# Four bank pairs for the last products of a two-attention kernel, and one VectorE tile fewer

## The chip, the cores and the metric

The kernel runs on one core of one Trainium2 chip. The metric is device microseconds of one execution. Before the change the median of three runs is 1860.64 us (1858.08 to 1861.57).

## The reference

Two attentions over the same input are mixed by a gate, token by token. Cut to what matters:

```python
B, S, D = 1, 2048, 512; H = 32; Dh = 16
g = sigmoid((x * gate_w).sum(-1))
# a: 32 query heads, one key head and one value head for all
a = softmax(einsum("bhqd,bkd->bhqk", x @ wq, x @ wk) * Dh**-0.5) @ (x @ wv), heads joined, @ wo_a
# b: 32 heads, each with its own keys and values
b = softmax(q @ k.T * Dh**-0.5) @ v per head, heads joined, @ wo_b
out = g * a + (1 - g) * b
```

All of it is float32. There are 2 x 32 heads with 2048 x 2048 scores each, and every score needs one exponential.

## The kernel before

**Work and its units.** The 64 heads form eight groups of eight (`groups`, alternately of a and b). A group has four *phases*: two halves of the tokens by two sets of four heads. A phase has 64 score tiles of 128x1024: PE makes them in 8 matmuls from K and Q tiles (`products`, two PSUM tiles `sc` in turn), and an exponential turns each into probabilities. Most exponentials run on ACT (`score`, tiles `prob`). Some run on VectorE (`chain`): the scores then go into a PSUM bank pair `pair`, and seven VectorE instructions follow, one that converts, two with bit masks, and four of a polynomial in place, on tiles `vec`. A chain holds three `vec` tiles while it runs, and its result stays in one until PE has read it. PE multiplies the probabilities with the values (`values`) into the other bank pair. When a phase is full, VectorE copies that bank pair to `raw` (`emptied`), ten small transfers bring numerators to `oT` and denominators to `dT` (`normalised`), and VectorE divides: a reciprocal (`over`), a multiplication (`times`), and a split into two float16 halves (`high` a cast, `low` a subtraction), which go to `o16`.

**Other products.** Between scores and values PE also works on *units*: projections to q, k and v of later groups, and output products (`o_unit`: four token tiles for each half of a group, 48 matmuls each when both sets of heads are in). An output product is gated by VectorE into a tile `sum` and added to the output in DRAM by POOL's queue. For the last group the output so far is read back into `late`, and VectorE adds the gated product to it in one instruction.

**What sets the order.** A planner in Python (`_Plan`) keeps a clock for each engine and writes the instructions out one by one. PE's next job is a score if ACT can take one, else values, a unit or the scores of a chain. A chain is begun when no unit is pressed for time (`hurry`, from each unit's due time), when enough `vec` tiles are free (`vector_job`), and when the phase has room (`pick`). So a unit that is due later leaves VectorE free for more chains, and each chain takes one exponential from ACT. Each engine then runs its own list in order.

**The end.** The last phase's division and the last output products stand behind the planner's loop, in a list of their own: in four steps of 128 tokens VectorE runs `over` and `times`, ACT `high` and POOL `low`; PE makes 24 matmuls, always into the same bank pair; VectorE adds the two halves of the gated product, and two queues (SP and ACT) store them.

```python
for t in range(4):
    if t < 3:
        c = (t + 1) * P
        over(c), times(c), high(c), low(c)
    for fn, _ in last[t].jobs:
        fn()
    last[t].finish(plan.pe)
```

Of the kernel before, what the change touches and what calls it, by code (L numbers as in the profile page):

```python
# [12 lines left out]
F32 = mybir.dt.float32  # L13
# [7 lines left out]
P = 128  # L21
# [26 lines left out]
TO_VEC, FROM_VEC, CHAINED = 255, 150, 130  # L48
X_JOB = 685
ISSUE, ISSUE_SP, LANDS, SUM_LANDS = 480, 600, 3200, 6500  # L50
PROBS, VECS = 6, 7


@with_exitstack
# [110 lines left out]
def _fast(ctx, tc, x, wq_a, wk_a, wv_a, wo_a, wqkv_b, wo_b, gate_w, out, flag):  # L165
# [36 lines left out]
    def by_tiles(outs, lhs, rhs, start, stop):  # L202


        for n in range(0, P, COLS):
            for i in range(2):
                nc.tensor.matmul(outs[n : n + COLS, i], lhs[i][rows(i), n : n + COLS], rhs[i][rows(i)],  # L207
                                 start=start, stop=stop)
# [122 lines left out]
    def kv_split(h, bank):  # L331


        pk = bank[:, :, : 4 * M].rearrange("p a (i m) -> p a i m", i=4)
        k32 = ops.tile([P, 2, 4, DH], F32, tag="k32", name=f"k32{h}", bufs=1)
        kn = sums[1][:, h].bitcast(F16).rearrange("p (i a b d) -> p i a b d", i=8, a=2, b=4)
        ts = slice(8 * h, 8 * h + 8)

        def take(queue=nc.sync, key=True, value=True):
            if key:  # L340
                nc.vector.tensor_scalar(k32, pk[:, :, :, :DH], UP ** -1, None, op0=ALU.mult)
            if value:
                for d in (0, 2 * DH):
                    v = vA[0][:, ts, d : d + DH].rearrange("p (e i) d -> p e i d", e=2)
                    nc.vector.tensor_scalar(v, pk[:, :, :, DH : 2 * DH], UP ** -2, None, op0=ALU.mult)
                swapped(vA[1][:, ts], vA[0][:, ts], queue)
                nc.vector.tensor_copy(z[:, ts].rearrange("p (e i) -> p e i", e=2), pk[:, :, :, 2 * DH])

        def halve():
            k8 = k32.rearrange("p e i d -> p (e i) d")  # L350
            nc.vector.tensor_copy(kn[:, :, 0, 0, :], k8)
            nc.vector.tensor_tensor(kn[:, :, 0, 2, :], k8, kn[:, :, 0, 0, :], op=ALU.subtract)
            nc.vector.tensor_copy(kn[:, :, 0, 1, :], kn[:, :, 0, 0, :])
            nc.vector.tensor_copy(kn[:, :, 0, 3, :], kn[:, :, 0, 2, :])
            nc.vector.tensor_copy(kn[:, :, 1], kn[:, :, 0])
        def top():
            absmax("k_a", h, k32.rearrange("p e i d -> p (e i) d"), AX.XY)

        return kn, take, halve, top
# [121 lines left out]
    def o_unit(n, half, t, qs, first, last):  # L481

        src, gi = groups[n]
        w, i = weights[src, gi, "o"], "ab".index(src)
        steps = [(q, a, b) for q in qs for a, b in PARTS]
        tt = [8 * half + t, 8 * half + 4 + t]
        mine = late[:, 4 * half + t]
        state = {}

        def job(k):  # L490
            q, a, b = steps[k]
            lhs = [o16s[n, half, q][:, a, t * P : (t + 1) * P]] * 2
            rhs = [w[e ^ (q // 2)][:, b] for e in range(2)]
            by_tiles(pair[1], lhs, rhs, k == 0, k == len(steps) - 1)

        def finish(end):
            def take(e):
                g = gate_up[:, i, tt[e] : tt[e] + 1]
                if n + 1 == len(groups):
                    nc.vector.scalar_tensor_tensor(mine[:, e], pair[1][:, e], g, mine[:, e], op0=ALU.mult, op1=ALU.add)  # L500
                    if last:
                        (nc.sync, nc.scalar)[e].dma_start(out[tt[e] * P : (tt[e] + 1) * P, :], mine[:, e])
                    return
                if e == 0:
                    state["sum"] = sums[state["turn"]]
                nc.vector.tensor_scalar(state["sum"][:, e], pair[1][:, e], g, None, op0=ALU.mult)  # L506

            def then(t):
                free["spare"] = t + FROM_VEC
                if n + 1 == len(groups):  # L510
                    return
                dst = out.rearrange("(h e t p) d -> h t p e d", h=2, e=2, p=P)[half, t_]
                if n == 0:
                    done = plan.on_sp([lambda: nc.sync.dma_start(dst, state["sum"])], t, ISSUE_SP)
                else:
                    done = plan.on_pool([lambda: nc.gpsimd.dma_start(dst, state["sum"], accum_op=ALU.add)], t, 1300)  # L516
                sum_free[state["turn"]] = done + SUM_LANDS

            t_ = t
            begin = end + TO_VEC  # L520
            if n + 1 < len(groups):
                state["turn"] = turn[0]
                turn[0] ^= 1
                begin = max(begin, sum_free[state["turn"]])
            for e in range(2):
                plan.vec(lambda e=e: take(e), 660, 1, begin, (), then if e else None)

        made = ready.get
        jobs = [(lambda k=k: job(k), PRODUCT) for k in range(len(steps))]
        due = 32 * (4 * n + 2 * half + 4)  # L530
        return _Unit(jobs, finish, lambda now: all(made(("o16", n, half, q), math.inf) <= now for q in qs)
                     and made(("wo", src, gi), math.inf) <= now and made("gates", math.inf) <= now
                     and (sum_free[turn[0]] <= now + 4000 if n + 1 < len(groups) else made("late", math.inf) <= now), lambda: starts_in(due), f"o{n}{half}{t}")
# [3 lines left out]
    def normalised(n, half, q, raw, now):  # L537

        src, gi = groups[n]
        ends = n + 1 == len(groups) and half and q  # L540
        o, d = (ops.tile([P, BLK], F32, tag=tag, name=f"{tag}{n}{half}{q}", bufs=1) for tag in ("oT", "dT"))
        queues = (nc.sync, nc.scalar, nc.gpsimd) if ends else (nc.sync,)
        moves = [(d, DH, 2 * DH, 0), (d, 5 * DH, 2 * DH, 2 * DH), (o, 0, DH, 0), (o, 3 * DH, 2 * DH, DH), (o, 7 * DH, DH, 3 * DH)]
        moves = [(*move, e) for part in (0, 2) for e in range(2) for move in moves[part : part + 2 + part // 2]]
        for m, (part, at, n_rows, to, e) in enumerate(moves):
            queues[m % len(queues)].dma_start(part[ROWS * e + to :][:n_rows], raw[at : at + n_rows, e])  # L546
        plan.sp = max(plan.sp, now) + len(moves) * ISSUE_SP
        o16 = ops.tile([P, 2, BLK], F16, tag="o16", name=f"o16{n}{half}{q}", bufs=3)
        o16s[n, half, q] = o16
        cut = P if ends else BLK // 2  # L550

        def over(c):
            nc.vector.reciprocal(d[:, c : c + cut], d[:, c : c + cut])  # L553

        def times(c):
            nc.vector.scalar_tensor_tensor(o[:, c : c + cut], o[:, c : c + cut], UP, d[:, c : c + cut], op0=ALU.mult, op1=ALU.mult)

        def high(c):
            (nc.scalar.copy if ends else nc.vector.tensor_copy)(o16[:, 0, c : c + cut], o[:, c : c + cut])  # L559

        def low(c):
            (nc.gpsimd if ends else nc.vector).tensor_sub(o16[:, 1, c : c + cut], o[:, c : c + cut], o16[:, 0, c : c + cut])

        if ends:
            tail.append((over, times, high, low))
            return
        due = now + 30000

        def then(end):
            ready["o16", n, half, q] = end + FROM_VEC  # L570

        for c in range(0, BLK, cut):
            a = plan.vec(lambda c=c: over(c), 1560, 3.5, now + 7700, (), None, due)
            b = plan.vec(lambda c=c: times(c), 330, 3.4, now + 12000, (a,), None, due)
            e = plan.vec(lambda c=c: high(c), 200, 3.3, 0.0, (b,), None, due)
            plan.vec(lambda c=c: low(c), 330, 3.2, 0.0, (e,), then if c else None, due)
# [132 lines left out]
    def emptied(t):  # L709
# [9 lines left out]

        def take():  # L720
            state["raw"] = ops.tile([P, 2, BLK], F32, tag="raw", name=f"raw{ph}", bufs=1)
            nc.vector.tensor_copy(state["raw"], full)  # L722

        def then(end):
            free[which] = end + FROM_VEC
# [496 lines left out]
        else:  # L1222
            plan.vector()

    over, times, high, low = tail[0]
    last = [o_unit(len(groups) - 1, 1, t, (2,), False, True) for t in range(4)]
    over(0), times(0), high(0), low(0)
    for t in range(4):
        if t < 3:
            c = (t + 1) * P  # L1230
            over(c), times(c), high(c), low(c)
        for fn, _ in last[t].jobs:
            fn()
        last[t].finish(plan.pe)
        for op in plan.ops:
            op.fn()
        plan.ops.clear()


def _sigmoid(nc, gate, z, scale):  # L1240
# [146 lines left out]
```

## Time and profile before

| | |
|---|---|
| median of three runs | 1860.64 us |
| the profiled execution: time, span | 1863.72 us, 1861.9 us |
| mean granted TensorE clock | 0.992 |
| busy: PE, VectorE (DVE), ACT, POOL | 1760.7, 1217.5, 1797.5, 392.0 us |
| exponentials of scores on ACT, on VectorE | 1944, 104 |
| first and last exponential on ACT start at | 32.2, 1829.4 us |

PE is TensorE's matmul, PEld its weight load, a name with q (SPq, ACTq) the sequencer that issues transfers. A number such as L622 is a line of the kernel; a group of rows is named by what it writes and reads, without buffer numbers. In a row of a timeline stand start, length, engine, line, operation, and in brackets the idle time before it with what ended it. Matmuls are pipelined and their ends are modelled, so PE's busy time is more than the work it must do. Idle time of an engine that is not the bottleneck costs nothing.

### The profile page before, as it was taken

Reading aid. Unit: us, or ns where it says so; the run is one execution under the profiler, and the core shown is the slowest. Engines: PE = TensorE matmul, PEld = TensorE weight load, DVE = VectorE, ACT = ScalarE, POOL = GpSimd, SP = SyncE. Lnnn points to the kernel's source line nnn. Section 1 sums busy time; section 2 is a strip of 40 time slices with the busy share of each in tenths; the row PEclk is TensorE's granted clock in tenths of the full one; section 3 lists DMA queues with packets and bytes.
Section 4 is the critical chain, followed back from the end, with each engine's and each line's share of the span. In section 5 each row is a group of like instructions: output and inputs, shape, how many; then the busy total and the mean of one; then the engine's idle time right before and its main releaser. Section 6 shows DMA issues by size and latency. Waiting matters only on the chain.

```text
span 1861.9 us, 97691 instructions
## 1 busy us (share of the span) xinstructions
PE 1760.7 (95%) x45403; PEld 859.8 (46%) x45403; DVE 1217.5 (65%) x1369; ACT 1797.5 (97%) x1959; POOL 392.0 (21%) x575
## 2 busy tenths in 40 slices
PE   9999999999999999999999999999999999998994
PEld 5544454444444444444444445444444444443441
DVE  4267323969686772678677684297868677349963
ACT  4999999999999999999999999999999999999993
POOL 4213103232031211412112320242202320130000
PEclk9999999999999999999999999999999999999997
DMA  5121212223142322412224240252313322234011
GB/s 146 41 60 43 82 32 55 82 57 57 32 79 40 66 49 59 83 35 54 43 50 75 51 80 21 51 97 48 57 40 54 65 53 45 51 66 124 24 49 59
DMA packets 75678, 109.69 MB, mean 59 GB/s; under 512 B 22256, under 2 KB 30672, under 8 KB 75264
## 3 DMA queue, kind: packets, MB, share of 16 engines
q0 software_dynamic: 27904, 44.24, 14.1%
q1 hardware_dynamic: 43920, 56.51, 11.9%
q8 instruction: 357, 5.85, 1.4%
q10 hardware_dynamic: 3440, 2.62, 0.4%
q14 instruction: 57, 0.47, 0.1%
HBM read 14.82 MB, written 33.55 MB: 26 GB/s over the span
## 4 chain that ended last, share of the span: by engine, by line
ACT 74%; PE 11%; issue 8%; DVE 5%; DMA 1%; SPq 1%; POOL 0%; ACTq 0%; DVEq 0%
ACT prob L622 74%; PE pair L663 5%; PE sc L608 3%; DVE vec L828 2%; PE pair L207 2%; DVE vec L816 1%; SPq L546 1%; DVE xT L500 0%; DVE dT L553 0%; DVE sum L506 0%; PE pt L294 0%; PE pair L294 0%; PE pair L457 0%; DVE vec L819 0%; DVE raw L722 0%
## 5 line engine op out<-in xcount | busy, mean ns | idle before, releaser
L622 ACT ACTIVATE prob<-sc 128x1024 f32<-128x1024 f32 x1932 | 1777.0, 1125 | 12.3 <-PE sc L608 10.4
L663 PE MATMUL pair<-prob,vA 64*32 64x512 f32 (+1 forms) x8168 | 521.8, 566 | 0.8 <-issue 0.8
L663 PE MATMUL pair<-prob,vB 64*32 64x512 f32 (+1 forms) x8112 | 521.7, 570 | 0.5 <-issue 0.5
L608 PE MATMUL sc<-Qb,K 64*32 64x512 f16 x7744 | 409.5, 381 | 47.0 <-ACT prob L622 38.7
L608 PE MATMUL sc<-Qa,kA 64*32 64x512 f16 x7808 | 409.5, 381 | 20.4 <-ACT prob L622 12.3
L608 PEld LDWEIGHTS <-K 64*32 64x32 f16 x8192 | 203.8, 90 | 422.9 <-issue 382.9
L608 PEld LDWEIGHTS <-kA 64*32 64x32 f16 x8192 | 202.9, 90 | 390.3 <-issue 349.9
L828 DVE SCALAR_TENSOR_TENSOR vec<-vec,vec 128x1024 f32<-128x1024 f32 x312 | 378.3, 1224 | 2.6
L663 PEld LDWEIGHTS pair<-prob,vA 64*32 64x32 f32 x8168 | 158.7, 105 | 23.7 <-issue 4.8
L663 PEld LDWEIGHTS pair<-prob,vB 64*32 64x32 f32 x8112 | 157.8, 105 | 22.2 <-issue 2.7
L816 DVE TENSOR_SCALAR vec<-pair 128x1024 int32<-128x1024 f32 x104 | 126.4, 1215 | 51.6 <-PE pair L608 49.3
L828 DVE SCALAR_TENSOR_TENSOR vec<-vec 128x1024 f32<-128x1024 f32 x104 | 131.3, 1263 | 1.2
L516 POOL DMA_DIRECT2D out_dram<-sum x48 | 60.1, 1253 | 340.7 <-DVE sum L506 330.8
L553 DVE RECIPROCAL dT<-dT 128x256 f32<-128x256 f32 (+1 forms) x66 | 111.4, 1693 | 28.2 <-DMA dT<-raw 28.2
L722 DVE COPY raw<-pair 128x1024 f32<-128x1024 f32 x32 | 39.2, 1224 | 115.3 <-PE pair L663 115.2
L506 DVE TENSOR_SCALAR sum<-pair,gate_up 128x512 f32<-128x512 f32 x112 | 79.2, 742 | 49.2 <-PE pair L207 49.1
L390 POOL DMA_DIRECT2D K<-hikb x64 | 31.1, 491 | 341.7 <-DVE hikb L431 340.9
L390 POOL DMA_DIRECT2D Qa<-hiqa x63 | 31.9, 511 | 335.7 <-DVE hiqa L431 316.9
L207 PE MATMUL pair<-w16ob,o 64*32 64x512 f16 x1536 | 66.1, 392 | 14.8 <-ACT o L559 6.9
L823 DVE TENSOR_SCALAR vec<-vec 128x1024 int32<-128x1024 int32 x104 | 78.1, 751 | 0.0
L819 DVE TENSOR_SCALAR vec<-vec 128x1024 int32<-128x1024 int32 x104 | 75.2, 723 | 1.4
L431 DVE TENSOR_SCALAR hivb<-pair 128x1024 f16<-128x1024 f32 x8 | 9.8, 1224 | 101.2 <-PE pair L207 101.2
(149 smaller groups left out, 1272.2 us busy)
## 6 DMA issues: line engine op xcount, KB each, us to landing
out_dram<-sum POOLq DMA_DIRECT2D x48, 512.0 KB, 6.1
dT<-raw SPq DMA_DIRECT2D x126, 64.0 KB, 3.0
vB<-vB SPq DMA_DIRECT2D x16, 384.0 KB, 3.8
out_dram<-sum SPq DMA_DIRECT2D x8, 512.0 KB, 3.8
xT<-out_dram SPq DMA_DIRECT2D x16, 256.0 KB, 5.0
oT<-raw SPq DMA_DIRECT2D x126, 32.0 KB, 2.9
oT<-raw SPq DMA_DIRECT2D x62, 64.0 KB, 2.9
vec<-in_A_x_dram SPq DMA_DIRECT2D x14, 256.0 KB, 4.9
```

The lines of the kernel that those rows point to most:

```text
L207: nc.tensor.matmul(outs[n : n + COLS, i], lhs[i][rows(i), n : n + COLS], rhs[i][rows(i)], start=start, stop=stop)
L390: fns.append(lambda q=queues[len(fns) % len(queues)], dst=dst, src=hilo[part][at]: q.dma_start(dst, src))
L506: nc.vector.tensor_scalar(state["sum"][:, e], pair[1][:, e], g, None, op0=ALU.mult)
L516: done = plan.on_pool([lambda: nc.gpsimd.dma_start(dst, state["sum"], accum_op=ALU.add)], t, 1300)
L553: nc.vector.reciprocal(d[:, c : c + cut], d[:, c : c + cut])
L608: nc.tensor.matmul(bank[a : a + COLS, hh], k[rows(hh), key : key + COLS], Q[src, gi, half, p][rows(hh), j * BLK : (j + 1) * BLK], start=Tr ...
L622: nc.scalar.activation(probs[u], sc, AF.Exp, scale=SCALE / (UP * UP))
L663: nc.tensor.matmul(pair[0][32 * k : 32 * k + 32, i, cols], v[rows(i)], probs[2 * m + k // 2][rows(i), hh, cols], start=first, stop=last)
L816: nc.vector.tensor_scalar(tile("p").bitcast(I32), pair[1], SCALE / (UP * UP) / math.log(2) * 2.0 ** 23, None, op0=ALU.mult)
L819: nc.vector.tensor_scalar(tile("m").bitcast(I32), tiles["p"].bitcast(I32), 0x7FFFFF, 125 << 23, op0=ALU.bitwise_and, op1=ALU.bitwise_or)
L823: nc.vector.tensor_scalar(tile("w").bitcast(I32), tiles["p"].bitcast(I32), 0x7F800000, 0x40000000 | LEAD, op0=ALU.bitwise_and, op1=ALU.bit ...
L828: nc.vector.scalar_tensor_tensor(p, m if i == 3 else p, VEC[i], m if i else w, op0=ALU.add, op1=ALU.mult)
```

## The change

Six edits. (1) VectorE's tiles `vec` are six, not seven; the input tiles that had borrowed them at the start use both `sum` tiles, and the scratch for k moves from `sum` to the places of `oT` and `dT`. (2) The due time of each output product is three phases later. (3) `o16` has six places, not three, since they wait longer for their product. (4) `low` runs on VectorE at the end too, not on POOL. (5) The copy of the last phase's bank pair is halved between VectorE and ACT. (6) The last list is written anew: each of the four token tiles has its own bank pair (both `pair` and both `sc`), VectorE's gated sums (`give`) stand between its divisions, and all eight stores go through SP's queue.

```diff
-PROBS, VECS = 6, 7
+PROBS, VECS = 6, 6
...
-        kn = sums[1][:, h].bitcast(F16).rearrange("p (i a b d) -> p i a b d", i=8, a=2, b=4)
+        kn = ops.tile([P, BLK], F32, tag=("oT", "dT")[h], name=f"kn{h}", bufs=1)
+        kn = kn.bitcast(F16).rearrange("p (i a b d) -> p i a b d", i=8, a=2, b=4)
...
-        due = 32 * (4 * n + 2 * half + 4)
+        due = 32 * (4 * n + 2 * half + 7)
...
-        o16 = ops.tile([P, 2, BLK], F16, tag="o16", name=f"o16{n}{half}{q}", bufs=3)
+        o16 = ops.tile([P, 2, BLK], F16, tag="o16", name=f"o16{n}{half}{q}", bufs=6)
...
-            (nc.gpsimd if ends else nc.vector).tensor_sub(o16[:, 1, c : c + cut], o[:, c : c + cut], o16[:, 0, c : c + cut])
+            nc.vector.tensor_sub(o16[:, 1, c : c + cut], o[:, c : c + cut], o16[:, 0, c : c + cut])
...
-            nc.vector.tensor_copy(state["raw"], full)
+            if ph == LASTS:
+                nc.vector.tensor_copy(state["raw"][:, 0], full[:, 0])
+                nc.scalar.copy(state["raw"][:, 1], full[:, 1])
+            else:
+                nc.vector.tensor_copy(state["raw"], full)
...
-    last = [o_unit(len(groups) - 1, 1, t, (2,), False, True) for t in range(4)]
-    over(0), times(0), high(0), low(0)
+    into = [pair[1], pair[0]] + [ps_s.tile([P, ACT, BLK], F32, tag="sc", name=f"end{t}") for t in range(2)]
+
+    def products_of(t):
+        for k, (a, b) in enumerate(PARTS):
+            lhs = [o16s[n, 1, 2][:, a, t * P : (t + 1) * P]] * 2
+            by_tiles(into[t], lhs, [w[e ^ 1][:, b] for e in range(2)], k == 0, k == len(PARTS) - 1)
+
+    def give(t, e):
+        tt, mine = 8 + 4 * e + t, late[:, 4 + t, e]
+        nc.vector.scalar_tensor_tensor(mine, into[t][:, e], gate_up[:, 1, tt : tt + 1], mine, op0=ALU.mult, op1=ALU.add)
+        nc.sync.dma_start(out[tt * P : (tt + 1) * P, :], mine)
+
+    over[0]()
+    times[0]()
     for t in range(4):
-        if t < 3:
-            c = (t + 1) * P
-            over(c), times(c), high(c), low(c)
-        for fn, _ in last[t].jobs:
-            fn()
-        last[t].finish(plan.pe)
-        for op in plan.ops:
-            op.fn()
-        plan.ops.clear()
+        high[t]()
+        if t < 3:
+            over[t + 1]()
+        elif t == 3:
+            give(1, 1)
+            give(2, 0)
+        low[t]()
+        products_of(t)
+        if t < 3:
+            times[t + 1]()
+        if t == 1:
+            give(0, 0)
+        if t == 2:
+            give(0, 1)
+            give(1, 0)
+    give(2, 1)
+    give(3, 0)
+    give(3, 1)
```

Two places show how the rows move, both on VectorE. The first is its list at the very end, from the copy of the last bank pair on. Here `L553`, `L556` and `L500` are the reciprocal, the multiplication and the gated sum. Before:

```order
L722 COPY raw_43191<-pair_82 128x1024
L553 RECIPROCAL dT_43194<-dT_43194 128x128
L556 SCALAR_TENSOR_TENSOR oT_43193<-oT_43193,dT_43194 128x128
L553 RECIPROCAL dT_43194<-dT_43194 128x128
L556 SCALAR_TENSOR_TENSOR oT_43193<-oT_43193,dT_43194 128x128
L500 SCALAR_TENSOR_TENSOR xT<-pair_82,gate_up,xT 128x512 x2
L553 RECIPROCAL dT_43194<-dT_43194 128x128
L556 SCALAR_TENSOR_TENSOR oT_43193<-oT_43193,dT_43194 128x128
L500 SCALAR_TENSOR_TENSOR xT<-pair_82,gate_up,xT 128x512 x2
L553 RECIPROCAL dT_43194<-dT_43194 128x128
L556 SCALAR_TENSOR_TENSOR oT_43193<-oT_43193,dT_43194 128x128
L500 SCALAR_TENSOR_TENSOR xT<-pair_82,gate_up,xT 128x512 x4
```

And from the third reciprocal on in the changed kernel, where `L554`, `L557`, `L563` and `L1243` are reciprocal, multiplication, subtraction and gated sum:

```order
L554 RECIPROCAL dT_43244<-dT_43244 128x128
L563 TENSOR_TENSOR o_43255<-oT_43243,o_43255 128x128
L557 SCALAR_TENSOR_TENSOR oT_43243<-oT_43243,dT_43244 128x128
L1243 SCALAR_TENSOR_TENSOR xT<-pair_82,gate_up,xT 128x512
L554 RECIPROCAL dT_43244<-dT_43244 128x128
L563 TENSOR_TENSOR o_43255<-oT_43243,o_43255 128x128
L557 SCALAR_TENSOR_TENSOR oT_43243<-oT_43243,dT_43244 128x128
L1243 SCALAR_TENSOR_TENSOR xT<-pair_82,gate_up,xT 128x512
L1243 SCALAR_TENSOR_TENSOR xT<-pair_83,gate_up,xT 128x512 x2
L1243 SCALAR_TENSOR_TENSOR xT<-end_43256,gate_up,xT 128x512
L563 TENSOR_TENSOR o_43255<-oT_43243,o_43255 128x128
L1243 SCALAR_TENSOR_TENSOR xT<-end_43256,gate_up,xT 128x512
```

The subtraction has come to VectorE, a gated sum stands two steps behind its products instead of right behind them, and the sums read four bank pairs in turn (`pair_82`, `pair_83` and two named `end`).

The second place is VectorE's list about two thirds through, in the phase (from one copy `raw` to the next) in which k and q of group b are projected. `L816`/`L821` is the first instruction of a chain, `L819`/`L824` and `L823`/`L828` are the masks, `L506`/`L507` the gated sum of an output product, and `hi`, `lo` halves of a projection. Before, from the middle of the phase:

```order
L216 TENSOR_REDUCE stats<-hikb_28091 128x1
L506 TENSOR_SCALAR sum_110<-pair_82,gate_up 128x512 x2
L431 TENSOR_SCALAR hiqb_28939<-pair_82 128x1024
L434 SCALAR_TENSOR_TENSOR loqb_28940<-pair_82,hiqb_28939 128x1024
L216 TENSOR_REDUCE stats<-hiqb_28939 128x1
L816 TENSOR_SCALAR vec_103<-pair_82 128x1024
L819 TENSOR_SCALAR vec_106<-vec_103 128x1024
L816 TENSOR_SCALAR vec_109<-pair_82 128x1024
L823 TENSOR_SCALAR vec_107<-vec_103 128x1024
L819 TENSOR_SCALAR vec_105<-vec_109 128x1024
```

In the changed kernel, from the start of that phase:

```order
L727 COPY raw_27967<-pair_82 128x1024
L554 RECIPROCAL dT_27970<-dT_27970 128x256
L432 TENSOR_SCALAR hiqb_28245<-pair_83 128x1024
L554 RECIPROCAL dT_27970<-dT_27970 128x256
L435 SCALAR_TENSOR_TENSOR loqb_28246<-pair_83,hiqb_28245 128x1024
L557 SCALAR_TENSOR_TENSOR oT_27969<-oT_27969,dT_27970 128x256 x2
L560 CAST o_27981<-oT_27969 128x256
L821 TENSOR_SCALAR vec_105<-pair_83 128x1024
L563 TENSOR_TENSOR o_27981<-oT_27969,o_27981 128x256
L824 TENSOR_SCALAR vec_104<-vec_105 128x1024
L821 TENSOR_SCALAR vec_106<-pair_83 128x1024
L828 TENSOR_SCALAR vec_107<-vec_105 128x1024
```

The projection of k is already over when the phase begins, the output products that stood between the projections have moved behind them, and two chains begin before any gated sum; four begin in this phase where two began. Over the whole program VectorE's chains are 112 where they were 104, and ACT's exponentials of scores 1936 where they were 1944.

More of the change, by code (lines that the diff above doesn't have):

```diff
@@ L1223, in _fast @@
             plan.vector()
-    over, times, high, low = tail[0]
-    last = [o_unit(len(groups) - 1, 1, t, (2,), False, True) for t in range(4)]
-    over(0), times(0), high(0), low(0)
+    over, times, high, low = ([lambda c=c * P, step=step: step(c) for c in range(4)] for step in tail[0])
+    n = len(groups) - 1
+    src, gi = groups[n]
+    w = weights[src, gi, "o"]
+    into = [pair[1], pair[0]] + [ps_s.tile([P, ACT, BLK], F32, tag="sc", name=f"end{t}") for t in range(2)]
[9 more added lines that the diff above has]
+    times[0]()
     for t in range(4):
+        high[t]()
         if t < 3:
-            c = (t + 1) * P
-            over(c), times(c), high(c), low(c)
-        for fn, _ in last[t].jobs:
-            fn()
-        last[t].finish(plan.pe)
-        for op in plan.ops:
-            op.fn()
-        plan.ops.clear()
+            over[t + 1]()
[14 more added lines that the diff above has]
+    give(3, 1)
 def _sigmoid(nc, gate, z, scale):
```

## The prediction

> **What bounds the kernel now.** I read the page first: who is busy, and the chain of work that ended last.
>
> ```profile
> PE 1760.7 (95%) x45403; PEld 859.8 (46%) x45403; DVE 1217.5 (65%) x1369; ACT 1797.5 (97%) x1959; POOL 392.0 (21%) x575
> ACT 74%; PE 11%; issue 8%; DVE 5%; DMA 1%; SPq 1%; POOL 0%; ACTq 0%; DVEq 0%
> ```
>
> PE and ACT both look full, so the chain must decide, and three quarters of it is ACT. Next I asked for ACT's own line and the chain's pieces in a quiet stretch.
>
> ```profile
> L622 ACT ACTIVATE prob<-sc x1932: 1017/1145/1157, 32.2 to 1829.4; 128x1024 f32<-128x1024 f32 x194
> L622 ACT ACTIVATE vec<-sc x12: 1018/1028/1100, 38.4 to 65.2; 128x1024 f32<-128x1024 f32 x12
> 1814.75 1.69 ACT prob L622 x2
> 1816.44 0.15 issue
> 1816.59 1.69 ACT prob L622 x2
> ```
>
> Two exponentials take 1816.59 - 1814.75 = 1.84 us, so ACT starts one every 0.92 us (neighbours overlap, which is why the listed 1.145 us is longer). From the first start to the last are 1797.2 us for 1943 intervals; at 0.917 that would be 1781.7. So 15.5 us are lost in small holes, the rest is pure ACT rate: from 32 to 1830 us, **the number of exponentials on ACT sets the time**. PE has room beside it:
>
> ```profile
> PE sc L608 <- ACT prob L622: 51.0, 143, 0.6
> ACT prob L622 <- PE sc L608: 10.4, 17, 2.9
> ```
>
> PE waited 51.0 us for ACT in 143 places, ACT only 10.4 us for PE in 17. After the last exponential comes a stretch of 32 us that nothing overlaps; its timeline is below.
>
> **The change, part by part.** *1. Exponentials.* By the order of instructions ACT has 1936 exponentials on scores where it had 1944, and VectorE 112 chains where it had 104. The eight come from later due times of the output products: they yield to chains where projections crowd, and most phases with two chains become phases with four. Saved on the path: 8 x 0.917 = 7.3 us. What VectorE pays:
>
> ```profile
> L816 DVE TENSOR_SCALAR vec<-pair 128x1024 int32<-128x1024 f32 x104 | 126.4, 1215 | 51.6 <-PE pair L608 49.3 <-ACT prob L622 1.9
> L819 DVE TENSOR_SCALAR vec<-vec 128x1024 int32<-128x1024 int32 x104 | 75.2, 723 | 1.4
> L823 DVE TENSOR_SCALAR vec<-vec 128x1024 int32<-128x1024 int32 x104 | 78.1, 751 | 0.0
> L828 DVE SCALAR_TENSOR_TENSOR vec<-vec,vec 128x1024 f32<-128x1024 f32 x312 | 378.3, 1224 | 2.6
> L828 DVE SCALAR_TENSOR_TENSOR vec<-vec 128x1024 f32<-128x1024 f32 x104 | 131.3, 1263 | 1.2
> ```
>
> One chain is (126.4 + 75.2 + 78.1 + 378.3 + 131.3) / 104 = 7.6 us, eight are 61 us. VectorE is idle 1861.9 - 1217.5 = 644 us, and most where the chains are few:
>
> ```profile
> 554.00:612.00 58.00, 57.40 (x1530) 28.21 (x1513) 35.88 (x38) 58.00 (x65) 12.63 (x22) 1.00 0.27 54
> 1134.00:1192.00 58.00, 55.87 (x1545) 29.17 (x1539) 22.00 (x28) 57.68 (x64) 9.05 (x17) 1.00 0.26 53
> 1598.00:1656.00 58.00, 55.90 (x1456) 27.99 (x1456) 13.84 (x17) 58.00 (x64) 10.15 (x20) 1.00 0.21 41
> ```
>
> (Columns: window, its length, then PE, PEld, DVE, ACT and POOL busy, the granted clock.) In 1134 to 1192 VectorE works 22.0 of 58 us: two more chains (15 us) fit. If that cover were gone, a late chain would hold PE's value products and then ACT. So 61 us of VectorE count for nothing, and 7.3 us stand.
>
> *2. Six tiles instead of seven, later due times, six places for normalised outputs.* No instruction is added; a seventh tile could only have let a chain start sooner, and the count of chains is the net of that. A VectorE write into a tile whose value products have not run would wait; behind it stand the copies that free TensorE's banks. Nothing in the trace bounds this well. It gains at most the 15.5 us of holes and can cost as much again; I take 0 and keep a third of it, 5 us, on both sides. The moved k scratch stands at the start and between single instructions whose number is unchanged: 0.
>
> *3. The last stretch.*
>
> ```profile
> 1831.75 1.22 DVE L722 COPY raw<-pair 128x1024 f32<-128x1024 f32 x1 [10.56 <-PE pair L663]
> 1835.91 0.95 DVE L553 RECIPROCAL dT<-dT 128x128 f32<-128x128 f32 x1 [2.94 <-DMA dT<-raw]
> 1837.86 0.29 DVE L556 SCALAR_TENSOR_TENSOR oT<-oT,dT 128x128 f32<-128x128 f32 x1 [1.00 <-DMA oT<-raw]
> 1838.07 0.94 DVE L553 RECIPROCAL dT<-dT 128x128 f32<-128x128 f32 x1
> 1838.19 0.30 ACT L559 CAST o<-oT 128x128 f16<-128x128 f32 x1 [7.62 <-DVE oT L556]
> 1838.54 1.05 PE L207 MATMUL pair<-w16ob,o 64*32 64x512 f16 x16 [6.86 <-ACT o L559]
> 1842.46 0.81 POOL L562 TENSOR_TENSOR o<-oT,o 128x128 f16<-128x128 f32 x2 [7.43 <-issue]
> 1842.93 0.63 PE L207 MATMUL pair<-w16ob,o 64*32 64x512 f16 x8 [3.34 <-POOL o L562]
> 1843.63 1.41 DVE L500 SCALAR_TENSOR_TENSOR xT<-pair,gate_up,xT 128x512 f32<-128x512 f32 x2 [4.29 <-PE pair L207]
> 1845.10 1.48 PE L207 MATMUL pair<-w16ob,o 64*32 64x512 f16 x24 [1.54 <-DVE xT L500]
> 1852.67 1.41 DVE L500 SCALAR_TENSOR_TENSOR xT<-pair,gate_up,xT 128x512 f32<-128x512 f32 x2 [1.60 <-PE pair L207]
> ...
> 24.66 1.09 ACT L1131 ACTIVATE hiqa<-pair 128x512 f16<-128x512 f32 x2 [9.12 <-PE pair L207]
> L562 DVE TENSOR_TENSOR o<-oT,o 128x256 f16<-128x256 f32 x62 | 25.3, 417 | 0.4
> ```
>
> Read the brackets: PE waits for POOL, DVE for PE, PE for DVE, one pair of banks passed to and fro. From 1837.86 to the end of the last 1.41 us, 1854.08, are 16.2 us.
>
> The copy of the last bank pair (1.22 us) becomes two halves side by side: a 128x512 operation on VectorE takes 1.41 / 2 = 0.71 us, on ACT 1.09 / 2 = 0.55. Saved: 0.5 us. ACT's half is queued only ahead of its own three transfers, which wait for the copy anyway.
>
> Then, with four bank pairs, VectorE need not wait for PE. Its work after the landing is four multiplications of 0.29, three reciprocals of 0.94 (the first still hides in the landing), four subtractions and eight gated sums of 0.705. A 128x128 subtraction on VectorE is not in the trace: it has one from both sides: half of the 128x256 one's 0.417 is 0.21, POOL's is 0.41 (0.81 for two). I take 0.27, near the 0.29 of VectorE's multiplication of that shape (four of them: 0.2 us less or 0.6 us more in all at the ends). Sum: 1.16 + 2.82 + 1.08 + 5.64 = 10.7 us. Does PE keep up? Of a group's 24 matmuls (1.48 us) sixteen need the cast alone and eight (0.5 us) the subtraction too. The first cast is over 0.65 us in, so sixteen end at 1.7; the subtraction is done at 0.29 + 0.94 + 0.27 = 1.5, and the eight end at 2.2 to 2.3. The first gated sum comes at 3.3, behind three multiplications, two reciprocals and two subtractions. Later groups have more room, and the last, eight matmuls behind the last subtraction, is covered by one sum of 0.7. ACT's casts (0.30) lie under reciprocals and sums. Saved: 16.2 - 10.7 = 5.5 us.
>
> The trace grants half the clock here, and the matmul rows above are at that rate:
>
> ```profile
> 1832.00:1838.00 6.00, 0.00 (x0) 0.00 (x0) 2.06 (x3) 0.00 (x0) 1.71 (x3) 0.90 0.32 87
> 1838.00:1842.00 4.00, 1.05 (x16) 0.15 (x16) 1.31 (x3) 0.60 (x2) 0.00 (x0) 0.50 0.00 0
> ```
>
> The Trainium skill, "TensorE: Matmul & The Clock Gate", section "What's actually happening", says that an idle window of about 3.4 us halves the clock and a busy one restores it; the 6 idle us and the 0.50 agree. By that rule the denser products could come back to full clock, and the sum would be about 0.2 us larger, since only the last eight matmuls are near the path.
>
> *4. Behind the last sum.* POOL no longer computes at the end.
>
> ```profile
> L562 POOLq MODIFY_POOL_CONFIG  x2: 49/49/49, 1835.1 to 1835.1; - x2
> L1382 POOLq DRAIN  x3: 52/107/10272, 1850.7 to 1861.6; - x3
> L1382 SPq DRAIN  x3: 7/7/7, 1858.0 to 1861.3; - x3
> 1848.09 0.34 ACTq L502 DMA_DIRECT2D out_dram<-xT  x1
> ```
>
> POOL changed its configuration at 1835.1 and its first subtraction began at 1842.46. After its last one it drained for 10.27 us, to 1861.0, while SP was through 4.0 us after the last sum, at 1858.1. The changed kernel leaves POOL with transfers alone, done some 13 us before the last sum, so a drain of 10.3 us ends before SP does. Saved: 1861.0 - 1858.1 = 2.9 us; bounds 0 and 2.9. All eight output transfers now go through SP's queue; at 0.34 us an issue and sums 0.7 us apart, none queues behind another: 0.
>
> The Trainium skill, "GPSIMD Engine Reference", section "Instruction dispatch", gives about 6 us for the first call after such a change of configuration; the trace has 7.4. By the page's figure the first subtraction would have come 1.4 us sooner and taking it away would be worth that much less; the measured number decides.
>
> Sum: 7.3 + 0.5 + 5.5 + 2.9 = **16.2 us**. The profiled execution took 1863.72 (span 1861.9 and 1.8 around it) and would take 1847.5. It lies 3.1 above the median of the runs, 1860.64, and from that median the forecast is **1844.4 us**.
>
> **The rivals.** *POOL still ends last.* The drain has no releaser in the trace; if it hangs on the end of the others and not on POOL's last work, 2.9 us stay: 1847.3. For it: nobody else drains so long. Against: it starts 0.6 us behind POOL's last subtraction. Chance 0.16.
>
> *PE becomes the bound where the chains were added.* In 554 to 612 PE is busy 57.40 of 58 us; if ACT merely waits longer, the eight exponentials bring nothing: 1844.4 + 7.3 = 1851.7. Against: PE's busy time is modelled, its matmul work is the same in number, and it waited 51.0 us for ACT. Chance 0.16.
>
> *Slower: six tiles tie VectorE to PE.* Two chains hold all six, so a third waits until PE has read one, and VectorE's copies wait behind it.
>
> ```profile
> 890.30 2.08 DVE vec L828
> ```
>
> That is the longest such stretch of a chain on the path so far. If half of the 28 phases or so that have chains got one, 14 x 2.08 = 29 us: 1873.5. It turns the sign at 16.2 / 28 = 0.58 us per phase. Against: VectorE hardly waits inside chains (2.6 and 1.4 us over the whole kernel in the rows above), and the phases with five chains stay at five. Chance 0.06.
>
> **How the numbers follow.** Forecast 0.62, the others 0.16, 0.16, 0.06. A measurement tells about 0.2%, 3.7 us, from no change. All cases but the last are faster by more: 0.94; of the last, 0.01 within and 0.05 slower. Range: below, 5 us fewer holes, 1839; above, 5 us more holes with POOL's 2.9 kept, or the second rival, 1853.
>
> **What would show it.** ACT with 1936 exponentials at 0.917 us and holes of 10 to 20 us in all; about 11 us between the first multiplication of the last stretch and the last gated sum, with no row of PE or DVE waiting a microsecond for the other; POOL's drain over before SP's. It is wrong if ACT's first start to last start is not 5 to 10 us shorter, if DVE waits for PE in the last stretch, or if VectorE waits inside chains by tens of us.

## The result and the profile after

The changed kernel takes 1848.5 us (median of four runs, 1848.0 to 1850.1) where the kernel before takes 1860.7: ratio 0.9938, 95% interval 0.9921 to 0.9955. That is 12.2 us less, inside the forecast range and 4.1 us short of the forecast. Its profiled execution took 1848.23 us, with a span of 1846.5.

The busy line of the page, ACT's own line, and two rows of the waits of the changed kernel:

```profile
PE 1756.4 (95%) x45419; PEld 856.0 (46%) x45419; DVE 1263.7 (68%) x1429; ACT 1789.2 (97%) x1952; POOL 396.2 (21%) x571
...
L623 ACT ACTIVATE prob<-sc x1924: 1017/1144/1171, 36.7 to 1823.5; 128x1024 f32<-128x1024 f32 x193
L623 ACT ACTIVATE vec<-sc x12: 1017/1028/1093, 42.8 to 69.8; 128x1024 f32<-128x1024 f32 x12
...
PE sc L609 <- ACT prob L623: 42.2, 120, 0.6
ACT prob L623 <- PE sc L609: 8.9, 12, 2.6
```

From the first exponential's start to the last one's are 1823.5 - 36.7 = 1786.8 us, 10.4 less than before. PE still waits for ACT in 120 places. But read the first number: the first exponential starts at 36.7, not at 32.2. So the span splits into three pieces that moved in different ways: start +4.5, middle -10.4, end 1846.5 - 1823.5 = 23.0 instead of 32.5, -9.5; together -15.4, the difference of the two spans.

The start, in the timeline of POOL, from the kernel before and then from the changed one:

```profile
0.73 0.20 POOL masks.py:197 MEMSET ident<- 128x128 f32 x1 [0.29 <-POOLq L1373]
1.23 0.29 POOL masks.py:199 TENSOR_SCALAR_AFFINE_SELECT ident<-ident 128x128 f32<-128x128 f32 x1 [0.29 <-POOL ident masks.py:197]
1.48 1.57 POOL L275 DMA_DIRECT2D prob<-in_gate_w_dram  x2
```

```profile
0.73 0.20 POOL masks.py:197 MEMSET ident<- 128x128 f32 x1 [0.29 <-POOLq L1402]
10.82 0.28 POOL masks.py:199 TENSOR_SCALAR_AFFINE_SELECT ident<-ident 128x128 f32<-128x128 f32 x1 [9.89 <-issue]
11.08 1.59 POOL L275 DMA_DIRECT2D prob<-in_gate_w_dram  x2
...
11.16 2.19 PE L294 MATMUL pt<-ident,vec 128*64 128x128 f32 x18 [5.10 <-POOL ident masks.py:199]
```

The same instruction, right behind POOL's memory sets, waits 9.89 us for nothing that the profile shows. It makes the identity matrix for the first transposes, and PE stands idle for it. Of the 9.6 us that it comes later, 4.5 reach the first exponential. The diff touches none of this.

The last stretch of the changed kernel, VectorE first, then what else matters:

```profile
1825.86 0.69 DVE L724 COPY raw<-pair 128x512 f32<-128x512 f32 x1 [10.56 <-PE pair L664]
1831.19 0.29 DVE L557 SCALAR_TENSOR_TENSOR oT<-oT,dT 128x128 f32<-128x128 f32 x1 [0.54 <-DMA oT<-raw]
1831.40 0.94 DVE L554 RECIPROCAL dT<-dT 128x128 f32<-128x128 f32 x1
1832.26 0.23 DVE L563 TENSOR_TENSOR o<-oT,o 128x128 f16<-128x128 f32 x1
1832.41 0.28 DVE L557 SCALAR_TENSOR_TENSOR oT<-oT,dT 128x128 f32<-128x128 f32 x1
1832.60 0.94 DVE L554 RECIPROCAL dT<-dT 128x128 f32<-128x128 f32 x1
...
1835.66 2.06 DVE L1243 SCALAR_TENSOR_TENSOR xT<-pair,gate_up,xT 128x512 f32<-128x512 f32 x3
1837.64 0.74 DVE L1243 SCALAR_TENSOR_TENSOR xT<-end,gate_up,xT 128x512 f32<-128x512 f32 x1
1838.30 0.29 DVE L563 TENSOR_TENSOR o<-oT,o 128x128 f16<-128x128 f32 x1
1838.50 2.07 DVE L1243 SCALAR_TENSOR_TENSOR xT<-end,gate_up,xT 128x512 f32<-128x512 f32 x3
1838.64 0.41 PE L207 MATMUL end<-w16ob,o 64*32 64x512 f16 x8 [1.82 <-DVE o L563]
...
1826.59 0.59 ACT L725 COPY raw<-pair 128x512 f32<-128x512 f32 x1 [1.91 <-DVE raw L724]
L1411 POOLq DRAIN  x3: 52/107/10272, 1830.0 to 1846.2; - x3
L1411 SPq DRAIN  x3: 7/7/7, 1845.6 to 1845.9; - x3
```

VectorE has no bracket of idle time after the landing: it runs through, and PE waits for it. ACT's half of the copy carries a bracket that was not forecast: it waited for VectorE's half.

### The profile page after: what moved, and what is told of

It is laid out like the page before. It is cut to its first block, busy times and chain, and to the rows that moved or that the text cites. A ratio compares the mean times of both kernels' runs of the same rounds, so it can differ in the third digit from the quotient of the medians.

```text
span 1846.5 us, 97759 instructions
## 1 busy us (share of the span) xinstructions
PE 1756.4 (95%) x45419; PEld 856.0 (46%) x45419; DVE 1263.7 (68%) x1429; ACT 1789.2 (97%) x1952; POOL 396.2 (21%) x571
## 3 DMA queue, kind: packets, MB, share of 16 engines
q1 hardware_dynamic: 44496, 57.56, 12.2%
## 5 line engine op out<-in xcount | busy, mean ns | idle before, releaser
L664 PE MATMUL pair<-prob,vB 64*32 64x512 f32 (+1 forms) x7968 | 510.5, 572 | 1.2 <-issue 1.2
L609 PE MATMUL sc<-Qb,K 64*32 64x512 f16 x7648 | 396.6, 380 | 41.1 <-ACT prob L623 32.2
L833 DVE SCALAR_TENSOR_TENSOR vec<-vec,vec 128x1024 f32<-128x1024 f32 x336 | 407.7, 1226 | 2.6
L821 DVE TENSOR_SCALAR vec<-pair 128x1024 int32<-128x1024 f32 x112 | 136.5, 1218 | 59.1 <-PE pair L609 58.9
L664 PEld LDWEIGHTS pair<-prob,vB 64*32 64x32 f32 x7968 | 153.2, 105 | 21.4 <-issue 2.8
L554 DVE RECIPROCAL dT<-dT 128x256 f32<-128x256 f32 (+1 forms) x66 | 111.6, 1696 | 46.7 <-DMA dT<-raw 46.7
L833 DVE SCALAR_TENSOR_TENSOR vec<-vec 128x1024 f32<-128x1024 f32 x112 | 139.7, 1247 | 1.3
L391 POOL DMA_DIRECT2D Qb<-hiqb x64 | 32.9, 518 | 321.7 <-DVE hiqb L432 320.7
L507 DVE TENSOR_SCALAR sum<-pair,gate_up 128x512 f32<-128x512 f32 x112 | 78.9, 743 | 16.1 <-PE pair L207 16.0
L824 DVE TENSOR_SCALAR vec<-vec 128x1024 int32<-128x1024 int32 x112 | 79.0, 706 | 1.6
L828 DVE TENSOR_SCALAR vec<-vec 128x1024 int32<-128x1024 int32 x112 | 79.7, 712 | 0.0
```

The lines of the kernel that those rows point to most:

```text
L391: fns.append(lambda q=queues[len(fns) % len(queues)], dst=dst, src=hilo[part][at]: q.dma_start(dst, src))
L609: nc.tensor.matmul(bank[a : a + COLS, hh], k[rows(hh), key : key + COLS], Q[src, gi, half, p][rows(hh), j * BLK : (j + 1) * BLK], start=Tr ...
L664: nc.tensor.matmul(pair[0][32 * k : 32 * k + 32, i, cols], v[rows(i)], probs[2 * m + k // 2][rows(i), hh, cols], start=first, stop=last)
L821: nc.vector.tensor_scalar(tile("p").bitcast(I32), pair[1], SCALE / (UP * UP) / math.log(2) * 2.0 ** 23, None, op0=ALU.mult)
L824: nc.vector.tensor_scalar(tile("m").bitcast(I32), tiles["p"].bitcast(I32), 0x7FFFFF, 125 << 23, op0=ALU.bitwise_and, op1=ALU.bitwise_or)
L828: nc.vector.tensor_scalar(tile("w").bitcast(I32), tiles["p"].bitcast(I32), 0x7F800000, 0x40000000 | LEAD, op0=ALU.bitwise_and, op1=ALU.bit ...
```

## The experiments

Each time is a median, each ratio is to the kernel before on the same chip, whose median was 1863.05 us beside the first four and 1863.67 beside the others.

**Theory:** the eight exponentials and the new end bring what was forecast, and something new, POOL's late mask instruction, takes 4.5 us back. Its cause would be the code that the execution before left in POOL: before the change ordinary subtractions were the last that POOL computed, now it is an all-reduce (a maximum over the 128 partitions, at 1714.7 us). **Rivals:** the new places of tiles delay the start; or it is a chance of one execution; and for the middle, fewer holes and not fewer exponentials.

### One POOL instruction behind the all-reduce

```diff
         nc.gpsimd.partition_all_reduce(highest, each, P, ReduceOp.max)
+        nc.gpsimd.tensor_sub(each, each, each)
```

> The changed kernel with one more instruction: right behind the all-reduce of the limits (about 1720 us in, POOL is idle for the next 110 us) POOL subtracts a 128x16 tile from itself; nobody reads the result. Theory (POOL's code at the start): the execution before leaves the all-reduce's code loaded in POOL, so the first instruction of the ordinary kind at the next start waits some 9.6 us; the extra subtraction brings the ordinary code back where POOL is idle. The first mask instruction then starts near 1.2 us, the first exponential near 32.2 instead of 36.7, and the time is 1848.5 - 4.5 = 1844.0 us. Rival (new tile places: two input tiles and the k scratch lie elsewhere): the start stays at 36.7 and the time at 1848.5. Rival (chance of that execution): the first exponential lies anywhere between, and the median of five rounds does not move.

Measured: 1842.5 us, ratio 0.9893 (0.9878 to 0.9908). Its mask instruction, its first exponentials, and the added instruction:

```profile
masks.py:199 POOL TENSOR_SCALAR_AFFINE_SELECT ident<-ident x1: 294/294/294, 1.2 to 1.2; 128x128 f32<-128x128 f32 x1
L623 ACT ACTIVATE prob<-sc x1924: 1016/1144/1170, 32.1 to 1820.7; 128x1024 f32<-128x1024 f32 x193
1720.19 0.20 POOL L1027 TENSOR_TENSOR each<-each 128x16 f32<-128x16 f32 x1 [7.10 <-issue]
```

An instruction 1720 us into the program moved the mask instruction at its start from 10.8 to 1.2 us. Within one execution that cannot be; it must act through the execution before. A trace holds one execution, so this step is inferred; whether POOL is instead set up when a program is loaded, differently for each, was not tried. The wait is still there, 7.10 us ahead of the added instruction, but at a place where POOL has nothing to do. This kernel beats both others.

### The subtraction on VectorE alone

```diff
-            (nc.gpsimd if ends else nc.vector).tensor_sub(o16[:, 1, c : c + cut], o[:, c : c + cut], o16[:, 0, c : c + cut])
+            nc.vector.tensor_sub(o16[:, 1, c : c + cut], o[:, c : c + cut], o16[:, 0, c : c + cut])
```

> The kernel before with one edit of the change alone: the last subtractions run on VectorE, not on POOL. 1944 exponentials as before, all tile places as before. Theory (POOL's code at the start): no ordinary POOL instruction follows the all-reduce any more, so the start is late: first exponential at 36.7, +4.5 us. At the end the first products come about 3.5 us sooner and POOL's drain no longer ends last, -1.8; together 1860.7 + 4.5 - 5.3 = 1859.9 us. Rival (new tile places): the first exponential stays at 32.2 and the time is 1860.7 - 5.3 = 1855.4. In both POOL's drain is 10.27 us long and ends before SP's.

Measured: 1863.0 us, ratio 0.9999 (0.9990 to 1.0008): nothing gained.

```profile
masks.py:199 POOL TENSOR_SCALAR_AFFINE_SELECT ident<-ident x1: 285/285/285, 11.1 to 11.1; 128x128 f32<-128x128 f32 x1
L622 ACT ACTIVATE prob<-sc x1932: 1017/1144/1157, 36.1 to 1834.9; 128x1024 f32<-128x1024 f32 x194
```

With every tile where it was, the start is late all the same (36.1), which removes the rival of the tile places. The end is 1861.4 - 1834.9 = 26.5 us, 6.0 less; the start gave back 3.9, and holes 1.6 in this execution.

### The main part alone

Edits (1) to (3) of the change on the kernel before:

```diff
-PROBS, VECS = 6, 7
+PROBS, VECS = 6, 6
...
-        due = 32 * (4 * n + 2 * half + 4)
+        due = 32 * (4 * n + 2 * half + 7)
```

> The kernel before with the three edits of the main part alone: six tiles with the moved k scratch, due times three phases later, six places for normalised outputs; the end is the old one. 1936 exponentials on ACT, 112 chains. Theory: eight exponentials are worth 8 x 0.917 = 7.3 us, the start stays at 32.2 because POOL still subtracts at the end: 1853.4 us. Rival (the main part also has fewer holes, 10.4 us between the two profiled executions): 1850.3. Rival (new tile places delay the start): first exponential at 36.7, 1857.9.

Measured: 1854.0 us, ratio 0.9956 (0.9943 to 0.9970), that is, by the ratio, -8.2 us (-5.6 to -10.6).

```profile
L623 ACT ACTIVATE prob<-sc x1924: 1015/1145/1173, 30.7 to 1820.4; 128x1024 f32<-128x1024 f32 x193
```

The start is early, at 30.7, though the tiles lie in their new places. The middle is 1789.7 us against 1797.2. The six places of `o16` were not tried by themselves.

### The end alone

```diff
-    last = [o_unit(len(groups) - 1, 1, t, (2,), False, True) for t in range(4)]
+    into = [pair[1], pair[0]] + [ps_s.tile([P, ACT, BLK], F32, tag="sc", name=f"end{t}") for t in range(2)]
```

with the rest of edits (4) to (6), on seven tiles and the old due times.

> The kernel before with the edits of the end alone: subtraction on VectorE, the halved copy, four bank pairs, stores on SP's queue. Seven tiles, old due times, 1944 exponentials. Theory: from the last exponential to the end 23.0 instead of 32.4 us, -9.4, and the late start, +4.5: 1860.7 - 4.9 = 1855.8 us. Rival (new tile places delay the start): start at 32.2, 1851.3.

Measured: 1860.0 us, ratio 0.9982 (0.9973 to 0.9991), that is -3.4 us (-1.7 to -5.0), where -4.9 was expected.

```profile
L622 ACT ACTIVATE prob<-sc x1932: 1012/1144/1158, 36.4 to 1835.0; 128x1024 f32<-128x1024 f32 x194
```

Start late at 36.4, end 1858.2 - 1835.0 = 23.2 us. Main part and end together, -8.2 - 3.4 = -11.6, make up the change within the intervals.

### The old due times with six tiles

```diff
-        due = 32 * (4 * n + 2 * half + 7)
+        due = 32 * (4 * n + 2 * half + 4)
```

> The changed kernel with one edit undone: the output products are due when they were before (the number 4, not 7). Six tiles, six places, the new end and the late start stay. Its order has 1950 exponentials on ACT and 98 chains: six tiles alone cost 6 chains against the kernel before, the later due times bring 14. Theory (the count of exponentials sets the middle): 14 x 0.917 = 12.8 us above the changed kernel, 1861.3 us where that one has 1848.5, no faster than the kernel before. Rival (fewer holes, not fewer exponentials, made the middle shorter): within 4 us of the changed kernel.

Measured: 1868.3 us, ratio 1.0023 (1.0014 to 1.0032), 0.2% slower than the kernel before; 17.6 us above the changed kernel on the same chip.

```profile
L623 ACT ACTIVATE prob<-sc x1938: 1016/1144/1171, 35.9 to 1843.8; 128x1024 f32<-128x1024 f32 x194
ACT prob L623 <- PE sc L609: 15.3, 20, 2.8
```

The later due times are worth more than the expected 12.8 us: the middle is 1807.9 us, 19.1 above that of the changed kernel's execution below. Fourteen exponentials are 12.8 of it; most of the other 6 are holes (ACT waited 15.3 us for PE, before the change 10.4, in the two profiles of the changed kernel 8.9 and 10.1). So on six tiles the later due times do two things: more chains, and fewer holes.

### The changed kernel again

No edit.

> The changed kernel itself, so that it stands on the same chip as the others of this call. Theory: late start (mask instruction near 10.8 us), 1848.5 us, 0.9938 of the kernel before, and the count of holes in its profile differs from the first profile by a few us, since they come with the execution.

Measured: 1850.7 us, ratio 0.9925 (0.9911 to 0.9938).

```profile
masks.py:199 POOL TENSOR_SCALAR_AFFINE_SELECT ident<-ident x1: 282/282/282, 10.7 to 10.7; 128x128 f32<-128x128 f32 x1
L623 ACT ACTIVATE prob<-sc x1924: 1017/1145/1171, 37.0 to 1825.8; 128x1024 f32<-128x1024 f32 x193
```

The late start is there again, so it is no chance. The middle is 1788.8 us, 2 more than in the first profile: holes vary by a few us from one execution to the next. The kernel with POOL's extra instruction stands at 0.9893 against 0.9925 here, 6 us better, of which the start is 37.0 - 32.1 = 4.9; the rest is within the intervals.

### The last stores on two queues

```diff
-        nc.sync.dma_start(out[tt * P : (tt + 1) * P, :], mine)
+        (nc.scalar if e and t > 1 else nc.sync).dma_start(out[tt * P : (tt + 1) * P, :], mine)
```

> The kernel with POOL's extra subtraction (start mended), and of the eight last stores the second halves of the last two token tiles go through ACT's queue. Theory (the 5.1 us behind the last sum, where 4.0 were forecast, are SP's wait for its last store and then its own list of waits): SP is through about 0.6 us sooner behind the last sum, 4.5 us. Rival (the landing itself takes so long from either queue): 5.1 stay.

The edit stands on the kernel with POOL's extra instruction. Measured in a single execution: 1843.8 us.

```profile
1834.29 2.06 DVE L1244 SCALAR_TENSOR_TENSOR xT<-end,gate_up,xT 128x512 f32<-128x512 f32 x3
L1412 SPq DRAIN  x3: 7/7/7, 1841.1 to 1841.4; - x3
```

The last sum ends at 1836.35 and SP drains from 1841.1 on: 4.8 us, where the changed kernel has 1840.57 and 1845.6, 5.0. Of the theory's 0.6 us half at most is there; the rival, that the landing takes so long from either queue, is nearer. The last store landed 3.7 us after its issue here, 4.0 in the changed kernel.

### The halves of the copy in two tiles

```diff
-                nc.scalar.copy(state["raw"][:, 1], full[:, 1])
+                nc.scalar.copy(state["half"], full[:, 1])
```

with `state["half"]` an idle sum tile, on the kernel with two store queues.

> As the kernel with two store queues, and the second half of the last copy goes to a tile of its own (an idle sum tile). In the changed kernel ACT's half waited for VectorE's half, 0.69 and then 0.59 us. Theory (they wait because they write one tile): both halves start together, the transfers leave 0.5 to 0.6 us sooner, and from the last exponential to the end it is 22.9 - 0.6 - 0.6 = 21.7 us; the median is about 1 us below the kernel with POOL's extra subtraction, 0.989 of the kernel before. Rival (both read one bank pair and cannot overlap): ACT's half still starts behind VectorE's.

Measured: 1844.5 us, ratio 0.9894 (0.9879 to 0.9909), no different from the kernel with POOL's extra instruction. From the last exponential to the end it was 23.4 us, not 21.7.

```profile
1823.78 0.59 ACT L726 COPY sum<-pair 128x512 f32<-128x512 f32 x1 [1.91 <-DVE raw L725]
```

A miss: ACT's half waits for VectorE's all the same, now that only the bank pair is common to them. Whether the program's wait or the memory itself holds the second reader was not tried.

## Why the prediction was right, and where it was not

**The exponentials: right, a little small.** 7.3 us were forecast. The main part alone gave 8.2 (5.6 to 10.6). In the profiles the middle took 1797.2, 1798.8 and 1798.6 us with 1944 exponentials (before, subtraction alone, end alone) and 1786.8, 1788.8, 1788.6, 1789.7, 1788.3 and 1789.6 with 1936: means 1798.2 and 1788.6, 9.6 apart. Eight exponentials are 7.3 of it. The other 2 would be fewer holes, which item 2 had put at zero with 5 either way; ACT's idle time just before its exponentials, 14.3 us on average with 1944 and 13.1 with 1936, shows 1.2 of them, and where the rest lies was not traced.

**The copy and the transfers: 0.8 us where 0.5 was forecast, and not for the reason given.** From the copy's start to the first multiplication it was 1837.86 - 1831.75 = 6.1 us and is 5.3. The halves do not run side by side (0.69, then 0.59); the first half's transfers leave while the second is copied.

**The interleaved end: 6.8 us where 5.5 was forecast.** From the first multiplication to the last sum's end are 1840.57 - 1831.19 = 9.4 us; the sum said 10.7. Its terms added the lengths of rows, but rows overlap: the reciprocal of 0.94 us is followed 0.86 later, three sums take 2.07 and not 2.12, a subtraction that follows a reciprocal shows 0.23. The order of events was as forecast, with no wait of VectorE. One sign failed: PE's last eight matmuls did wait over a microsecond for VectorE (1.82 us), which costs nothing, as VectorE sets the pace. The windows of the changed kernel show the clock come back while PE is busy:

```profile
1832.00:1834.00 2.00, 2.00 (x48) 0.48 (x36) 2.00 (x7) 0.38 (x2) 0.00 (x0) 0.50 0.00 0
1836.00:1838.00 2.00, 0.82 (x24) 0.15 (x16) 2.00 (x4) 0.08 (x1) 0.00 (x0) 0.92 0.42 153
```

The third column from the end is the granted clock: 0.50, then 0.92 after some 4 us of nearly unbroken products (from 1831.87 on). The last eight matmuls took 0.41 us in this execution where 0.63 stood before. The Trainium skill, "TensorE: Matmul & The Clock Gate", section "What's actually happening", says that a busy window of about 3.4 us restores the clock, and the trace agrees. It is not so in every execution: in the kernel with the halves in two tiles these matmuls took 0.63 us again, at 0.50, though PE had idled only 1.88 us, and the last three sums took 2.25 us instead of 2.07. So it is worth the 0.2 us of the step, no more.

**Behind the last sum: 1.9 us where 2.9 was forecast.** POOL's drain was again 10.272 us, from 1830.0 on, and over before SP's: the first rival is out. But from the last sum to SP's drain are 5.0 us, not 4.0. The step at fault is "none queues behind another: 0" for the eight stores. It priced their issue (0.34 us) and not what they move, 256 KB each. One line of the windows before, then one of the windows after, and the eight stores' landings in the changed kernel (least, median, most):

```profile
1846.00:1850.00 4.00, 2.06 (x40) 0.54 (x25) 3.13 (x6) 0.59 (x2) 0.78 (x2) 0.50 0.52 193
...
1838.00:1840.00 2.00, 0.41 (x8) 0.11 (x8) 2.00 (x5) 0.00 (x0) 0.00 (x0) 0.93 0.93 345
...
DMA to landing us min/median/max: 2.6/3.5/4.0
```

The last two columns are the busy share of the DMA engines and GB/s. With the sums only 0.66 us apart, the engines stay full: 345 GB/s here and 384 over the next 2 us, where before, from 1844 on, no 2 us average more than 262. The last store lands 4.0 us after its issue, where it landed after 2.9. Behind that landing SP is through its own list in 0.8 us in both kernels (1857.2 to 1858.0, 1844.8 to 1845.6). A second queue leaves the engines as full (360 and 369 GB/s) and gives back 0.3 us. No run spread the stores out to test this further.

**What failed: the sum has no term for the start.** Its one word on the start, "The moved k scratch stands at the start and between single instructions whose number is unchanged: 0", holds for the scratch (the main part alone starts at 30.7). But item 4 priced the removal of POOL's last subtractions at the end only. They also, by the experiments, left POOL ready for the next execution, and taking them away cost 3.9 to 4.9 us at the start (two runs with one edit each, in both directions). The prediction had the sign in its rows: MODIFY_POOL_CONFIG at 1835.1 and 7.4 us until the first subtraction. It asked what goes when that switch goes, and not where the switch would be made instead.

Put together from the two first profiles: -10.4 in the middle, -9.5 at the end, +4.5 at the start, -15.4; forecast were 16.2. That the two are so near is in part luck: the middle brought 3.1 more than its term, the interleaved end 1.3 and the copy 0.3 more, the stretch behind the last sum 1.0 less, and the start took 4.5 that no term had. The medians moved by 12.2, since the profiled execution of before was 3.0 us above its median and the one after was not.

The second rival (PE becomes the bound) is out: PE still waits for ACT, 42.2 us in 120 places, and the middle is shorter. The third (six tiles tie VectorE down) is right in its sign for six tiles alone, not in its mechanism: in the polynomial's rows VectorE waits 3.9 us over the whole changed kernel (3.8 before), but six tiles alone cost 6 chains, and with the late start and more holes that kernel is 1.0023 of before; the later due times pay for it. Its price was read from 2.08 us as the longest stretch of a chain on the path; the same view has a row of two operations with 2.27 us at 1786.98, which would make it 14 x 2.27 = 32 us, not 29.

## What to carry to other kernels

Where an engine needs its code changed, the question is not only what the change costs where it stands, but where it will stand when that work is gone: at the start of the next execution it may be on the path, in an idle stretch it is free. Where stores are brought closer together, price what they move and not only their issue. Split a span into start, middle and end by one engine's first and last instruction before adding terms; three effects of opposite sign hid in one difference here. Sum a row of operations by the distance of their starts, not by their lengths.

## What the runs showed of the hardware

POOL's state seems to outlive an execution. When the last that POOL computed was an all-reduce, the mask instruction starts at 10.4 to 11.1 us (five profiles); when ordinary work came last, at 1.2 (five profiles). The start of the program is the same in both: two MODIFY_POOL_CONFIG, of 11 ns each, stand ahead of the mask. The Trainium skill, "GPSIMD Engine Reference", section "Instruction dispatch", speaks of about 6 us for a first call after new code is loaded; measured here are 7.0 to 7.4 us inside the program and 9.5 to 10.1 at its start, and the measurement decides. Memory sets and transfers of POOL do not need it: the memory set ahead of the mask ran at 0.73 us in either case, and behind the all-reduce of the changed kernel POOL's transfer of the last half starts at 1827.47, 0.3 us after ACT's copy ends. And POOL drained for 10.27 us (once 10.32) at the end of every program here, whenever its last work was, so work on POOL in the last 10 us sets the end, as it did before the change (POOL's drain over at 1861.0, SP through at 1858.0).
